# First heads' value products ahead of the next unit's update, with a VectorE fence behind the carried products

## The chip, the cores and the metric

One core of a Trainium2 chip runs the kernel. The metric is device time in microseconds of one execution. Engines are TensorE (PE for its matmuls, PEld for its weight loads), VectorE (DVE), ScalarE (ACT), GpSimd (POOL) and SyncE (SP, which here only issues DMAs). The granted clock is TensorE's, as the profile gives it.

## The reference

Retention attention (a causal, decaying linear attention without softmax) and then a gated linear unit whose gate is a causal convolution. Batch 8, 8 heads, 576 positions, head dimension 64, model width 512, five convolution taps; all inputs and the output are float32.

```python
scores = scale * np.matmul(q, k.transpose(0, 1, 3, 2))
Dmat = np.where(rel >= 0, gamma[:, None, None] ** rel[None, :, :], 0.0)
attn = np.matmul(scores * Dmat[None, :, :, :], v)
x = attn.transpose(0, 2, 1, 3).reshape(B, S, H * D)
...
for k in range(K):
    gate_pre += conv_w[k][None, None, :] * xp[:, k:k + S, :]
gate = 1.0 / (1.0 + np.exp(-gate_pre))
return gate * (x @ w_val) @ w_out
```

## The kernel before

The decay is taken apart: `gamma ** (i - j)` is a factor of the query row and one of the value row (`gin` on the values as they are cast, `gout` on the result), so what stands between the two matmuls is a plain 0/1 mask.

Work is cut into 18 units. Units 0 to 15 are "full": 256 positions of one batch element, two units to each element (`cu` is 0 or 1), each with two chunks `c` of 128 positions. Units 16 and 17 are "tail": the last 64 positions of four batch elements each. Heads are taken in pairs `pr` of 0 to 3; `hf` 0 means pairs 0 and 1 (the first heads), `hf` 1 pairs 2 and 3. Matmuls of a unit's attention use 64 x 64 quarters of the TensorE array, four after each other on four different quarters (`QUAD`).

For one unit the steps are:

- `turn_halves`: TensorE turns keys and queries, ScalarE copies them to `kq0` and `kq1`, one for each half of the heads.
- `scores(u, hf)`: 16 matmuls of a half into PSUM, in tile "s" for half 1, and in two tiles "v" for half 0.
- `masks(u, hf)`: VectorE multiplies by the mask into `p0` or `p1` (line 356 for one wide product, line 352 for two narrow ones, one for each "v" tile).
- `carried(u, odd)`: products of the queries with the state of the chunks before (`s1`, `s2` and the like), accumulated into the output banks `o0` and `o1`. A unit with `cu` 0 has no state for its chunk 0, so it makes half as many.
- `values(u, hf)`: 16 matmuls of `p` with the values of the heads of that half, accumulated into the same banks.
- `take_x`: VectorE multiplies the banks by `gout` and writes them to `xg`.
- `update(u)`: 32 short matmuls of keys and values into PSUM tile "s" (the bank that `scores` of half 1 had), ScalarE copies them out, and GpSimd adds them up to the next state (`states`).
- `conv`, `gate_values`, `project`, `store`: the convolution into tile "a" with its sigmoid on ScalarE, `value` (8 matmuls in each of two "v" tiles, written `v<-xg,wvb` in the profile) times the gate on VectorE, the output projection into "v" tiles, and the output DMA.

PSUM tile "v" has two buffers; "s", "a", "o0" and "o1" have one each. `p0` has two buffers, `p1` one.

The schedule is written by hand (`manual_schedule`): each engine runs its instructions in the order in which the program makes them, and semaphores are put in where tiles are shared. After a lead-in that differs, the loop at line 770 runs 14 phases, n = 4 to 17, each with parts of several units: the second half of unit n's scores and its values, the first half of unit n + 1's scores and its update, the gate and projection of unit n - 1, and loads, casts and turns of later units. `bring` issues loads, each behind a small copy on VectorE or ScalarE that touches the tile. Where the order of the program matters here:

- `carried(n, 1)` is made inside `scores(n, 1)`, after its first four matmuls.
- `masks(n, 1)` comes ahead of `masks(n + 1, 0)` on VectorE.
- `update(n + 1)` is made only where unit n + 1 is full, so in phases 4 to 14.
- `values(n, 1)` waits for `p1`; `values(n, 0)` needs only `p0`, which the phase before has made.

`fence` (line 398) is an existing helper that reads one column of an output bank; the lead-in uses it three times with VectorE. `fill` (line 151) makes small matmuls ahead of the loop until the count of matmuls stands at a given place in a block of 127.

Of the kernel before, what the change touches and what calls it, by code (L numbers as in the profile page):

```python
# [13 lines left out]
F32 = mybir.dt.float32  # L14
# [7 lines left out]
def kernel(  # L22
# [10 lines left out]
    nc = tc.nc  # L33
# [3 lines left out]
    P = 128  # L37
    NP = H // 2
# [22 lines left out]
    small = ctx.enter_context(tc.tile_pool(name="small", bufs=1))  # L61
# [7 lines left out]
    units = [("full", b, c) for b in range(B) for c in range(NC2)]  # L69
# [5 lines left out]
    half = (lo, hi)  # L75
    QUAD = ((0, 0), (1, 1), (0, 1), (1, 0))

    with tc.manual_schedule():
# [249 lines left out]
        def scores(u, hf, between=None, pool=None):  # L328

            if pool is ps_v:  # L330
                s = [pool.tile([P, 2, 2, P], F32, name="v") for par in range(2)]
            else:
                st = (pool or ps_s).tile([P, 2, 2, 2, P], F32, name="a" if pool else "s")
                s = [st[:, par] for par in range(2)]
            t = kqt[u][hf]
            for prl in range(2):
                for r in range(2):
                    for (c, par) in QUAD:
                        matmul(s[par][half[c], prl, r, :], lhsT=t[half[par], 0, prl, r, c, :],
                                         rhs=t[half[par], 1, prl, :, c, :],  # L340
                                         start=True, stop=True, skip_group_check=True)
                    if between and prl == 0 and r == 0:
                        between()
            sps[u, hf] = s if pool is ps_v else st

        def masks(u, hf):
            m = mask if units[u][0] == "full" else mask_t
            p = pp.tile([P, 2, 2, 2, P], BF16, name=f"p{hf}", bufs=2 - hf)
            mrow = m.rearrange("p r a -> p (r a)").unsqueeze(1)
            if isinstance(sps[u, hf], list):  # L350
                for par in range(2):
                    nc.vector.tensor_tensor(p[:, par].rearrange("p l r a -> p l (r a)"),  # L352
                                            sps[u, hf][par].rearrange("p l r a -> p l (r a)"),
                                            mrow.to_broadcast([P, 2, W]), op=ALU.mult)
            else:
                nc.vector.tensor_tensor(p.rearrange("p e l r a -> p (e l) (r a)"),  # L356
                                        sps[u, hf].rearrange("p e l r a -> p (e l) (r a)"),
                                        mrow.to_broadcast([P, 4, W]), op=ALU.mult)
            pt[u, hf] = p

        ops, state = {}, {}
        opened = set()

        def first(u, c, par):
            new = (u, c, par) not in opened
            opened.add((u, c, par))
            return new

        def out_banks(u):
            if u not in ops:  # L370
                ops[u] = [ps_o.tile([P, NP, P], F32, name=f"o{c}") for c in range(2)]
            return ops[u]

        def carried(u, odd, chs=(0, 1)):

            kind, b, cu = units[u]
            o = out_banks(u)
            for pr in range(NP):
                t = kqt[u][pr // 2]
                for c in chs:  # L380
                    par = c ^ odd
                    rows = half[par]
                    if kind == "full":
                        st = state.get((b, 2 * cu + c))
                        if st is None:
                            continue
                        matmul(o[c][rows, pr, :], lhsT=st[rows, pr, :],
                                         rhs=t[rows, 1, pr % 2, :, c, :],
                                         start=first(u, c, par), stop=False, skip_group_check=True)
                    else:  # L390
                        for i in range(2):
                            st = state[b + 2 * c + i, 4]
                            cs = slice(i * 32, i * 32 + 32)
                            matmul(o[c][rows, pr, :].rearrange("p (r a) -> p r a", r=2)[:, :, cs],
                                             lhsT=st[rows, pr, :], rhs=t[rows, 1, pr % 2, :, c, cs],
                                             start=first(u, c, par), stop=False, skip_group_check=True)

        def fence(u, rows, c, eng=None):
            t = small.tile([P, 1], F32, name="fence", bufs=2)
            (eng or nc.scalar.copy)(t[rows], ops[u][c][rows, NP - 1, 0:1])  # L400

        def values(u, hf):
            vb = bf[u]["v"]
            o = out_banks(u)
            p = pt[u, hf]
            for prl in range(2):
                pr = 2 * hf + prl
                for r in range(2):
                    for (c, par) in QUAD:
                        matmul(o[c][half[par], pr, :], lhsT=vb[half[c], 2 * pr + par, r, :],  # L410
                                         rhs=p[half[c], par, prl, r, :], start=first(u, c, par),
                                         stop=(r == 1), skip_group_check=True)
# [20 lines left out]
        def update(u, own=False, now=True):  # L433
            kind, b, cu = units[u]
            if kind != "full":
                return
            kb, vb = bf[u]["k"], bf[u]["v"]
            if own:
                xy = [ps_v.tile([P, 512], F32, name="v") for c in range(2)]
            else:  # L440
                xyt = ps_s.tile([P, 2, 512], F32, name="s")
                xy = [xyt[:, c] for c in range(2)]
            for pr in range(NP):
                for r in range(2):
                    for (c, par) in QUAD:
                        h = 2 * pr + par
                        matmul(xy[c][half[par], pr * 64:pr * 64 + 64], lhsT=kb[half[c], r, h, :],
                                         rhs=vb[half[c], h, r, :], start=(pr == 0 and r == 0), stop=(pr == NP - 1 and r == 1),
                                         skip_group_check=True)
            xf = stp.tile([P, 2, NP, 64], F32, name="xf")  # L450
            if own:
                for c in range(2):
                    nc.scalar.copy(xf[:, c].rearrange("p o d -> p (o d)"), xy[c][:, 0:NP * 64])
            else:
                nc.scalar.copy(xf.rearrange("p c o d -> p c (o d)"), xyt[:, :, 0:NP * 64])  # L455


            xfs[u] = xf
            if now:
                states(u)  # L460
# [130 lines left out]
        def gate_values(n, e):  # L591
            value(n, 0, e)
            gated(n, 0, e)
# [40 lines left out]
        warm(1, 512, ps_s)  # L634
        values(0, 1)
        fence(0, lo, 1, dve)
        turn(1, ps_v, 0)
        take_part(1, 0, act)
        take_x(0, (0,))
        carried(0, 1)  # L640
        carried(0, 0)
        turn(1, ps_v, 1)
# [127 lines left out]
        for n in range(4, NU):  # L770
            def bring(name, u, i, eng):
                if u < NU:
                    load_half(name, u, i, eng)

            nxt = n + 1 < NU
            carried(n, 0)
            scores(n, 1, lambda: carried(n, 1))
            masks(n, 1)
            conv(n - 1, 0)
            bring("v", n + 3, 0, act)  # L780
            if nxt:
                scores(n + 1, 0, pool=ps_v)
                masks(n + 1, 0)
                update(n + 1)
            bring("v", n + 3, 1, act)
            values(n, 1)
            values(n, 0)
            gate_values(n - 1, 0)
            bring("k", n + 3, 1, dve)
            gate_values(n - 1, 1)  # L790
            bring("q", n + 3, 1, dve)
            take_x(n, (0,))
            take_x(n, (1,))
            bring("k", n + 4, 0, dve)
            if n + 2 < NU:
                cast1("v", n + 2)
                cast_half("k", n + 2, 1)
                cast_half("q", n + 2, 1)
            if n + 3 < NU:
                cast_half("k", n + 3, 0)  # L800
                cast_half("q", n + 3, 0)
            if nxt:
                turn_halves((n + 1, 1), *([(n + 2, 0)] if n + 2 < NU else []))
            bring("q", n + 4, 0, act)
            project(n - 1, 0, 0, 2)
            project(n - 1, 0, 1, 2 - n % 2)
            store(n - 1)
# [34 lines left out]
```

## Time and profile before

| | us |
|---|---|
| Three runs: median (lowest to highest) | 160.12 (159.75 to 162.49) |
| The profiled execution, its own time | 159.02 |
| Its span in the profile | 157.3 |
| Its mean granted TensorE clock, share of full | 0.999 |
| The loop's first phase begins; the last one's convolution of unit 16 begins | 42.8; 140.6 |

Times in the profile count from the start of the span. In lists of groups and in the timeline a line reads: start, duration, engine, line of the kernel, operation, written tile <- read tiles, shapes, count, and in brackets the idle time of that engine before it with what ended it. All matmuls carry line 146, that of a helper that counts them, so they are told apart by their tiles: `o<-kq,s` are carried products, `s<-kq` and `v<-kq` scores of half 1 and half 0, `s<-vb,kb` the update, `o<-p,vb` the values. The chain of waits lists the work that ended last, in order of time. The list of waits reads: who waited, for whom, total us, times, longest.

### The profile page before, as it was taken

To read this page: it belongs to the slowest core of one execution; us is meant where nothing else is said; L and a number is where in the kernel's file an instruction comes from. 1 tells how busy PE (TensorE), PEld (TensorE's weight loads), DVE (VectorE), ACT (ScalarE), POOL (GpSimd) and SP (SyncE) were. 2 spreads that over 40 slices of the span, in tenths; PEclk is the share of its full clock that TensorE was granted. 3 is DMA by queue.
4 is the path that set the end of the run, shared out by engine and by line. 5 is a ranking of instruction groups with operands and counts; after the bars stand their busy time and mean duration, and the time that the engine had idled before them with its cause. 6 is when DMAs were issued, how large, how long until landed. Compare 5 with 4: busy or idle time off the path is not lost.

```text
span 157.3 us, 8008 instructions
## 1 busy us (share of the span) xinstructions
PE 145.8 (93%) x3461; PEld 115.3 (73%) x3461; DVE 105.2 (67%) x214; ACT 93.4 (59%) x164; POOL 102.4 (65%) x166
## 2 busy tenths in 40 slices
PE   6977989989999999999999999999999999998960
PEld 2456667868788878877878788887878887876720
DVE  5786887693676867667768686767667676765340
ACT  6895664697846574747484848484656637252510
POOL 7679669397969695959596877869695842500000
PEclk9999999999999999999999999999999999999999
DMA  4999999999989999998999899899778872302135
GB/s 117 347 347 342 324 290 333 325 310 308 351 276 292 300 352 363 321 315 234 305 264 314 249 322 285 262 314 267 213 230 241 262 236 108 137 17 121 36 101 133
DMA packets 62561, 40.37 MB, mean 257 GB/s; under 512 B 2346, under 2 KB 59710, under 8 KB 62526
## 3 DMA queue, kind: packets, MB, share of 16 engines
q1 hardware_dynamic: 62400, 39.59, 82.1%
q8 instruction: 27, 0.44, 1.2%
q10 hardware_dynamic: 126, 0.27, 0.7%
q14 instruction: 8, 0.07, 0.1%
HBM read 30.42 MB, written 9.44 MB: 253 GB/s over the span
## 4 chain that ended last, share of the span: by engine, by line
PE 80%; DVE 8%; DMA 3%; ACT 2%; issue 1%; SPq 1%; POOL 1%; POOLq 0%; DVEq 0%
PE v L146 45%; PE a L146 19%; PE o L146 10%; PE s L146 7%; DVE p L356 3%; DMA fv<-in_v_dram 2%; DVE p L352 2%; SPq L586 1%; DMA out_dram<-ob 1%; DVE z L547 1%; DVE kq L323 1%; ACT ob L562 1%; POOL wob L243 1%; DVE xg L421 1%; ACT gate L527 1%
## 5 line engine op out<-in xcount | busy, mean ns | idle before, releaser
L319 ACT COPY kq<-a 128x1024 bf16<-128x1024 bf16 x26 | 25.0, 1015 | 28.0 <-PE a L146 28.0
L146 PE MATMUL v<-xg,wvb 128*128 128x256 bf16 x288 | 34.8, 273 | 0.3
L146 PE MATMUL v<-wob,z 128*128 128x256 bf16 (+1 forms) x209 | 32.9, 305 | 1.2 <-POOL wob L243 0.6
L547 DVE TENSOR_TENSOR z<-gate,v 128x512 bf16<-128x512 f32 x34 | 23.3, 686 | 14.0 <-PE v L146 11.5
L356 DVE TENSOR_TENSOR p<-s,mask 128x1024 bf16<-128x1024 f32 x17 | 20.8, 1223 | 17.1 <-PE s L146 17.1
L146 PEld LDWEIGHTS <-wvb 128*128 128x128 bf16 x288 | 26.7, 97 | 5.2 <-issue 0.2
L264 POOL TENSOR_TENSOR vb<-fv,gin 128x512 bf16<-128x512 f32 x28 | 28.6, 1042 | 0.0
L146 PEld LDWEIGHTS <-z 128*128 128x128 bf16 x217 | 20.3, 98 | 9.2 <-issue 1.7
L421 DVE TENSOR_TENSOR xg<-o,gout 128x512 bf16<-128x512 f32 x32 | 22.3, 736 | 4.5 <-PE o L146 4.4
L527 ACT ACTIVATE gate<-a 128x1024 f32<-128x1024 f32 x17 | 17.4, 1024 | 12.6 <-ACT ob L562 6.7
L146 PE MATMUL a<-xg,dg 64*64 64x256 bf16 x720 | 24.3, 270 | 0.6 <-DVE xg L421 0.3
L562 ACT COPY ob<-v 128x512 f32<-128x512 f32 x34 | 18.6, 581 | 5.1 <-PE v L146 5.1
L146 PEld LDWEIGHTS <-dg 64*64 64x64 bf16 x720 | 20.0, 106 | 1.4 <-issue 0.7
L146 PEld LDWEIGHTS <-kb 64*64 64x64 bf16 (+1 forms) x656 | 15.9, 107 | 5.0 <-DVE p L356 2.0
L271 POOL CAST kb<-fk 128x512 bf16<-128x512 f32 x28 | 17.0, 612 | 0.1
L146 PEld LDWEIGHTS <-kq 64*64 64x64 bf16 x576 | 15.6, 106 | 2.0 <-issue 1.7
L352 DVE TENSOR_TENSOR p<-v,mask 128x512 bf16<-128x512 f32 x24 | 15.4, 685 | 1.0
L478 POOL TENSOR_TENSOR mid<-run,xf 128x256 f32<-128x256 f32 x8 | 5.8, 726 | 13.5 <-ACT xf L455 12.3
L271 POOL CAST qb<-fq 128x512 bf16<-128x512 f32 x22 | 13.5, 614 | 0.1
L146 PE MATMUL o<-p,vb 64*64 64x128 bf16 x576 | 12.3, 218 | 0.9 <-DVE p L356 0.5
L146 PEld LDWEIGHTS <-s 64*64 64x64 bf16 x256 | 8.2, 107 | 6.2 <-issue 3.4
L146 PE MATMUL s<-kq 64*64 64x128 bf16 x304 | 12.2, 222 | 0.4 <-DVE kq L323 0.3
(98 smaller groups left out, 197.2 us busy)
## 6 DMA issues: line engine op xcount, KB each, us to landing
out_dram<-ob SPq DMA_DIRECT2D x16, 512.0 KB, 4.5
fk<-in_k_dram SPq DMA_DIRECT2D x28, 256.0 KB, 4.5
fq<-in_q_dram SPq DMA_DIRECT2D x28, 256.0 KB, 4.6
fv<-in_v_dram SPq DMA_DIRECT2D x28, 256.0 KB, 4.6
wkc<-in_k_dram SPq DMA_DIRECT2D x2, 512.0 KB, 5.0
wqc<-in_q_dram SPq DMA_DIRECT2D x2, 512.0 KB, 5.5
wvc<-in_v_dram SPq DMA_DIRECT2D x2, 512.0 KB, 5.9
wvf<-in_moe_w_val_dram SPq DMA_DIRECT2D x4, 256.0 KB, 4.9
```

The costliest lines, as they stand in the source:

```text
L146: return f(*a, **k)
L243: eng(wob[:, o, :], wof[o])
L264: nc.gpsimd.tensor_tensor(b[n][:, hs].rearrange("p h r d -> p (h r) d"), f.rearrange("p h (r d) -> p (h r) d", r=2), gin[:, units[u][2], h ...
L271: (eng or nc.gpsimd.tensor_copy)(b[n][:, :, hs].rearrange("p r h d -> p h r d"), f.rearrange("p h (r d) -> p h r d", r=2))
L319: nc.scalar.copy(kqt[u][hf].rearrange("p i l r c a -> p (i l r c a)"), ps[:, at].rearrange("p i l r a -> p (i l r a)"))
L352: nc.vector.tensor_tensor(p[:, par].rearrange("p l r a -> p l (r a)"), sps[u, hf][par].rearrange("p l r a -> p l (r a)"), mrow.to_broadcas ...
L356: nc.vector.tensor_tensor(p.rearrange("p e l r a -> p (e l) (r a)"), sps[u, hf].rearrange("p e l r a -> p (e l) (r a)"), mrow.to_broadcast ...
L421: nc.vector.tensor_tensor(x[:, b, :, PAD + i0:PAD + i0 + P].rearrange("p o (a r) -> p o r a", r=2), o[c].rearrange("p o (r a) -> p o r a", ...
L478: nc.gpsimd.tensor_tensor(mid, state[b, "run"], xf[:, 0], op=ALU.add)
L527: nc.scalar.activation(t, cps[j, i], AF.Sigmoid)
L547: nc.vector.tensor_tensor(zsb[j][:, 2 * e + ss[0]:2 * e + ss[-1] + 1, :], gsb[j, i][e], vps[j, i, e], op=ALU.mult)
L562: (eng or nc.scalar.copy)(outs[u][:, r], o)
```

## The change

`carried` runs over the pairs and the chunks in reverse, so that its last product goes to pair 0. A new `fence_first(n)`, made between the scores and the masks of half 1, has VectorE copy one column of pair 0 of the bank and the partitions that this last carried product writes. In the loop, `values(n, 0)` moves from behind `values(n, 1)` to a place ahead of `update(n + 1)`. `carried` is used in the lead-in too; the fence and the move are in the loop alone.

```diff
-            for pr in range(NP):
+            for pr in reversed(range(NP)):
                 t = kqt[u][pr // 2]
-                for c in chs:
+                for c in reversed(chs):
                     par = c ^ odd
                     rows = half[par]
...
+        def fence_first(u):
+            c = 1 if units[u][0] == "full" and units[u][2] == 0 else 0
+            rows = half[1 - c]
+            t = small.tile([P, 1], F32, name="fence", bufs=2)
+            nc.vector.tensor_copy(t[rows], ops[u][c][rows, 0, 32:33])
...
             carried(n, 0)
             scores(n, 1, lambda: carried(n, 1))
+            fence_first(n)
             masks(n, 1)
             conv(n - 1, 0)
             bring("v", n + 3, 0, act)
             if nxt:
                 scores(n + 1, 0, pool=ps_v)
                 masks(n + 1, 0)
+            values(n, 0)
+            if nxt:
                 update(n + 1)
             bring("v", n + 3, 1, act)
             values(n, 1)
-            values(n, 0)
             gate_values(n - 1, 0)
```

## The prediction

> **What bounds the kernel now.** I read the page first: one core, granted clock full in all 40 slices, and TensorE (PE) holds the chain that ended last.
>
> ```profile
> PE 145.8 (93%) x3461; PEld 115.3 (73%) x3461; DVE 105.2 (67%) x214; ACT 93.4 (59%) x164; POOL 102.4 (65%) x166
> ...
> PE 80%; DVE 8%; DMA 3%; ACT 2%; issue 1%; SPq 1%; POOL 1%; POOLq 0%; DVEq 0%
> ```
>
> So only what TensorE waits for can be won, and anything that delays it is lost in full. Next came the waits between 43 and 140 us, where thirteen of the fourteen loop phases (n = 4 to 17) lie; two rows matter.
>
> ```profile
> PEld L146 <- issue: 4.5, 12, 0.4
> PEld L146 <- DVE p L356: 2.0, 11, 0.2
> ```
>
> The first is the step from the last 512-wide projection to the carried products (row by row, 11 of the 12) and is not touched. The second is the target: in each of the 11 phases that have an update (n = 4 to 14) the weight loads stand 0.18 us before it, because the update overwrites the bank that the mask product p1 of `masks(n, 1)` still reads. One phase, n = 6, in the timeline; the last line is from a later window of the same phase:
>
> ```profile
> 58.35 1.22 DVE L356 TENSOR_TENSOR p<-s,mask 128x1024 bf16<-128x1024 f32 x1 [1.20 <-PE s L146]
> ...
> 59.14 0.46 PE L146 MATMUL v<-kq 64*64 64x128 bf16 x16
> ...
> 59.62 0.33 PEld L146 LDWEIGHTS <-kb 64*64 64x64 bf16 x32 [0.18 <-DVE p L356]
> 59.62 0.45 PE L146 MATMUL s<-vb,kb 64*64 64x64 bf16 x32
> 59.66 0.69 DVE L352 TENSOR_TENSOR p<-v,mask 128x512 bf16<-128x512 f32 x1
> ...
> 60.45 0.28 PE L146 MATMUL v<-xg,wvb 128*128 128x256 bf16 x1
> ```
>
> p1 ends at 59.57 and the update starts 0.05 later. The line at 59.66 is the first half of `masks(n + 1, 0)`, call it pv1; it ends at 59.66 + 0.69 = 60.35. It frees the first of the two PSUM tiles "v", which the value product (v<-xg,wvb) at 60.45 needs. That second gate is 0.10 ahead of its user now. How close a user can follow, phase 16 shows, where there is no update (its chain):
>
> ```profile
> 134.56 0.02 issue
> 134.58 0.70 DVE p L352
> 135.29 0.04 issue
> 135.33 0.71 PE v L146 x5
> ```
>
> There the value product already waits for pv1, and starts 0.05 us after its end.
>
> **The weight-load row or the matmul row.** The matmul row hides most of this stall: the last score product runs to 59.60 and the update's first starts at 59.62, 0.02 us of idle PE a phase, 0.2 over 11 phases, against 2.0 by the weight loads. The Trainium skill, "Perfetto Trace Analysis", section "Identifying the Most-Contended Engine", says that matmul busy time is a bad measure since matmuls are pipelined, and that weight-load busy is the better one; the trace agrees (2.0 against 0.2), and by the matmul row alone the regular phases' term below would be at most 0.2.
>
> **The change part by part.**
> *Values first, update after.* In the new order TensorE has, after the scores of unit n + 1, 16 value products of the first heads that need only p0, written one phase earlier. Worked on phase 6: the last score product starts at 59.60 - 0.22 = 59.38; the 32 value products of now run 0.62 us, less the last one's 0.22, so 0.40 of issue, 0.20 a half. First half from 59.41 to 59.61; update from 59.62 (p1's release is 59.62 too) with 0.45 - 0.20 = 0.25 of issue, to 59.88; second half to 60.09; then the step to the value product, which takes 0.15 now (60.30 to 60.45): 60.24. TensorE alone would gain 60.45 - 60.24 = 0.21. But pv1 does not move: it starts 0.06 after the end (59.60) of the very score products that it masks, and those are ahead of the edit. So the value product starts at 60.35 + 0.05 = 60.40: a gain of 0.05, with 0.16 of slack left ahead of the gate. What is late next is pv1.
> Nine phases (4, 5, 6, 8 to 12, 14): 9 x 0.05 = 0.45.
> Phases 7 and 13 have besides a stall put down to nothing ("issue"), in 7 within the update, in 13 (0.14) at the start of the values:
>
> ```profile
> 67.19 0.26 PEld L146 LDWEIGHTS <-kb 64*64 64x64 bf16 x20
> 67.85 0.10 PEld L146 LDWEIGHTS <-kb 64*64 64x64 bf16 x1 [0.39 <-issue]
> 67.85 0.50 PEld L146 LDWEIGHTS <-vb 64*64 64x64 bf16 x32
> 68.44 0.11 PEld L146 LDWEIGHTS <-wvb 128*128 128x128 bf16 x2
> ```
>
> I read it as the instruction stream running dry (queue q8 carries 27 instruction transfers, and the kernel's own `fill` reckons with blocks of 127 matmuls): it then ends at 67.85 whatever the order. By the count it falls some 16 products earlier in the work, mid-update, so half an update, half the values and the step follow: 67.85 + 0.13 + 0.02 + 0.20 + 0.15 = 68.35 against 68.44. About 0.1 each, 0.2.
> Phases 15 and 16 have no update; their value product hangs on pv1 today: 0. Phase 17 has neither update nor pv1:
>
> ```profile
> 142.19 0.64 PE L146 MATMUL o<-p,vb 64*64 64x128 bf16 x32 [0.22 <-DVE p L356]
> ...
> 142.76 0.28 PE L146 MATMUL v<-xg,wvb 128*128 128x256 bf16 x1
> ```
>
> All 32 wait for p1 there; now 16 run ahead, and the value product comes at 142.19 + 0.20 + 0.15 = 142.54: 0.22.
> *The fence.* Fourteen VectorE copies of one column. The nearest row is the fence that the kernel has already, same shape, same banks (nanoseconds least, median, most; first and last start):
>
> ```profile
> L400 DVE COPY fence<-o x3: 129/134/151, 11.6 to 24.2; 64x1 f32<-64x1 f32 x3
> ```
>
> Behind it on VectorE stand p1, pv1 and the rest of the phase, and TensorE waits for p1 and pv1. The last carried product of phase 6 starts at 57.90 and ends at 58.12, so the fence runs 58.18 to 58.31; p1 cannot start before 58.35, when its scores release it, and VectorE is idle for 1.20 us before. Phase 7: 65.62 + 0.06 + 0.13 = 65.81 against 65.85. Cost 0 from below (it frees nothing). From above, if it is released only with the last score, 0.13 a phase on p1 and the update; the value product would still be ready at 60.24 + 0.13 = 60.37, under the gate's 60.40, and pv1's start at 59.66 has 0.09 (p1's end to pv1's start) plus the 0.08 by which back-to-back VectorE products overlap. I take 0; it costs from about 0.16 a phase on. The first half of the values waits for the fence, done 1.1 us before it is needed.
> *Reverse order of the carried products.* As many products; the first one now needs the second half of the turned queries, the second output bank free, and the newest state. In phase 7 it starts at 64.93; ScalarE's copy of that half ends near 64.33, `take_x` ends at 64.44, GpSimd's state is done at 63.0. Cover 0.5 us, cost 0; without it, at most the four or eight products that stood ahead, 0.1 a phase.
> *What moves with it.* `values` issues no DMA, so SP, ScalarE and GpSimd keep their order. The update ends at nearly the same time; its ScalarE copy waits for the gate activation anyway (59.49 + 1.03 = 60.52).
> Sum: 0.45 + 0.20 + 0.22 = 0.87 us. The profiled execution, 157.3 of span and 159.02 in all, becomes 158.15; the median of the runs shown is 160.12, 1.10 above it, and becomes 159.25, say **159.2**. That is 0.5%, where this kernel's runs (159.75 to 162.49) tell 2% from nothing.
>
> **Rivals.**
> A. *pv1 gates nothing* (the value product gets another tile, or pv1 starts earlier). Then nine phases give 0.21 each, 1.9; 7 and 13 0.2; 15 and 16 the 0.45 each that pv1 costs them; 17 0.22: 3.2 us, 156.9. For it, only that TensorE is ready; against it, phase 16. Chance 0.06.
> B. *The gate takes all*: the value product starts 0.10 after pv1 as today, the 0.15 step is paid after the gate, or the gain is lost among the runs. Only 17 is left: 159.9. Nothing in phases 15 and 16 speaks for it. Chance 0.17.
> C. *Slower: the instruction stream.* The crossing of phase 7 lies at nearly the same count in 5, 9, 11 and 13, and the new order reaches it about 0.13 us earlier (67.25 for 67.38). It decides if the instructions are then not there. A stall of 0.49 as in 7 costs 0.49 - 0.16 (slack to the gate) = 0.33 in 5, 9 and 11, and half as much in 13: 1.2 us, less the 0.87: 160.4. If the other crossings, in the convolution and the projection, begin to stall at 0.49 too, seven more cost 3.4: 163.8. Against: those in 5, 9 and 11 show no gap now. Chance 0.17, of it 0.05 for over 2%.
> D. *The fence is dear*: released later than the last score. At 0.45 a phase (0.29 past the slack, 14 times) 4.1 - 0.9 = 3.2 us slower, 163.3. Nothing shows such a wait. Chance 0.03.
> That the change does not do what it says: the order is written out by hand and the engines keep it, so no chance of its own.
>
> **How the numbers follow.** Forecast 0.57, A 0.06, B 0.17, C 0.17, D 0.03. The time is the forecast's. The range reaches from 158.0 (the forecast with twice the gain in 7, 13 and 17 and a run level like the profiled one's) to 160.9 (C without its far end, and half a us of run level); A and the ends of C and D are left out. Faster by over 2% (under 156.9): A, which lands on that bound, 0.05. Slower by over 2% (over 163.3): C's far end and D, 0.08. Within: 0.87.
>
> **What would show it.** Right: the waits of weight loads on p (L356) shrink from 2.0 us to near nothing in phases 4 to 14, and a wait on p (L352) appears ahead of the value product, as in 134.58; the period of a phase without issue stalls falls by about 0.05; the fence ends before p1's release, and p1's start after the last score stays at 0.06. Wrong: p1 later than that (D), value products starting well before pv1's end (A), gaps put down to issue in phases 5, 9 and 11 (C).

## The result and the profile after

The change made the kernel slower, by 3.3%: 166.6 us median (164.87 to 172.73, six runs) against 160.72 for the kernel before in as many (159.75 to 162.49), a ratio of 1.033 with a 95% interval of 1.026 to 1.041. Medians here and below are of all executions, ratios of those within 1.5% of each kernel's fastest. The profiled execution took 166.19 us, its span 164.4 against 157.3, 7.1 us more. The forecast was 159.2.

From the page of the changed kernel, the span, the busy times and the chain by engine:

```profile
span 164.4 us, 8017 instructions
PE 143.0 (87%) x3444; PEld 115.5 (70%) x3461; DVE 107.6 (65%) x228; ACT 93.9 (57%) x164; POOL 103.3 (63%) x166
...
PE 70%; DVE 12%; issue 7%; DMA 4%; SPq 1%; POOL 1%; ACT 1%; DVEq 0%; POOLq 0%
```

The weight loads are as many and as long as before, so TensorE has the same work. What is new is "issue" in the chain, 7% where it was 1%: time in which TensorE waits for nothing that the profile shows. The list of waits of the loop (43 to 147 us; who waited, for whom, total us, times, longest) says where:

```profile
PEld L146 <- issue: 11.9, 16, 1.9
...
PE s L146 <- issue: 4.2, 4, 1.4
...
PE o L146 <- issue: 1.8, 1, 1.8
PE v L146 <- issue: 1.4, 1, 1.4
...
PE v L146 <- DVE p L352: 0.4, 1, 0.4
PE a L146 <- issue: 0.3, 1, 0.3
```

The target is hit: the 2.0 us that weight loads stood for p (L356) are gone from the list. But matmuls stand 4.2 + 1.8 + 1.4 + 0.3 = 7.7 us for "issue". The kernel before has one such row in its loop (43 to 140 us):

```profile
PE s L146 <- issue: 0.3, 1, 0.3
```

The 7.4 us more cover the whole loss of span. Four of these gaps are in the update of the odd phases 7, 9, 11 and 13, one in the values of phase 15, one in the projection of phase 4. Phase 9 in the timeline:

```profile
85.14 0.20 PEld L146 LDWEIGHTS <-kb 64*64 64x64 bf16 x13
...
86.84 0.24 PEld L146 LDWEIGHTS <-kb 64*64 64x64 bf16 x19 [1.50 <-issue]
86.84 0.35 PE L146 MATMUL s<-vb,kb 64*64 64x64 bf16 x19 [1.39 <-issue]
```

The update stops behind its 13th matmul and goes on 1.5 us later. In the trace's order of weight loads the four gaps of phases 9 to 15 begin at numbers 1883, 2266, 2649 and 3032, each 383 apart: three blocks of 256 instructions, as a matmul is two instructions (766) and two more per pair of phases come in, of which below. The 27 instruction transfers on queue q8 (0.44 MB) are 16 KB each, and TensorE's 6940 instructions (3461 weight loads, as many matmuls, 18 semaphore instructions) make 27 blocks of 256. So, as far as the counts tell, TensorE waits for its instructions, which was rival C's place, with gaps two to four times the 0.49 us that it reckoned with.

An even phase shows the forecast at work. Phase 6 after the change:

```profile
60.32 1.23 DVE L356 TENSOR_TENSOR p<-s,mask 128x1024 bf16<-128x1024 f32 x1
...
61.34 0.22 PE L146 MATMUL o<-p,vb 64*64 64x128 bf16 x2
61.36 0.22 PE L146 MATMUL v<-kq 64*64 64x128 bf16 x1
61.38 0.42 PE L146 MATMUL o<-p,vb 64*64 64x128 bf16 x14
...
61.60 0.46 PE L146 MATMUL s<-vb,kb 64*64 64x64 bf16 x32
61.64 1.29 DVE L352 TENSOR_TENSOR p<-v,mask 128x512 bf16<-128x512 f32 x2
...
62.38 0.38 PE L146 MATMUL v<-xg,wvb 128*128 128x256 bf16 x2
```

From the start of the last score product (61.36) to the value product it is 1.02 us, where it was 60.45 - 59.38 = 1.07: 0.05 less, and the value product starts 0.05 behind pv1's end (61.64 + 0.69 = 62.33). Phases 8, 10, 12 and 14 show the same 1.02.

**Where the extra instructions come from.** At the first carried product of phase 9 the trace of the changed kernel has three waits: the weight load (82.90) waits for GpSimd, its matmul for ScalarE, and ahead of both a semaphore instruction of TensorE's sequencer (82.24) waits for VectorE. No weight load and no matmul in either trace waits for more than one engine.

In reverse order this product is the first to need three things at once: the newest state (GpSimd), the output bank (VectorE) and the second half of the turned queries (ScalarE). Forward, the first product needs only the state and the bank, one wait for the weight load and one for the matmul, and ScalarE's wait falls on a later product. The trace of before has no semaphore instruction of TensorE in the loop; this one has 11, at the start of phases 5 to 15 (50.47, 59.13, 66.40, 74.99, 82.24 and so on), each 0.45 to 1.7 us ahead of its carried product. Ten of them begin 0.04 us behind the end of `take_x` on VectorE (82.20 in phase 9): the sequencer was held until the output bank was free. The first comes later, behind the gap of phase 4. That gap, 1.4 of the 7.7 us, stands ahead of all 11, and they do not explain it. The page's count fits: 8017 - 8008 = 9 is 14 fences, these 11 and one more in the lead-in, less 17 matmul records that are missing.

**What happens to the instruction transfers.** Instruction DMAs in a stretch from just before the crossing in phase 8's projection, first of the kernel before (78.6 to 79.4), then of the changed one (80.7 to 84.3):

```profile
DMA packets 432, 0.23 MB, mean 286 GB/s; under 512 B 16, under 2 KB 431, under 8 KB 431
...
q8 instruction: 1, 0.02, 10.4%
```

```profile
DMA packets 1806, 0.92 MB, mean 257 GB/s; under 512 B 57, under 2 KB 1798, under 8 KB 1806
## 3 DMA queue, kind: packets, MB, share of 16 engines
q1 hardware_dynamic: 1806, 0.92, 85.6%
```

Before, the transfer starts within 0.8 us; after, there is none in 3.6 us. By the count of instructions, the crossings in the projections of phases 6, 8, 10, 12 and 14 were followed by the start of a transfer after 2.4, 0.6, 0.6, 0.6 and 0.5 us before, and after 2.9, 3.6, 3.1, 2.8 and 3.7 us with the change, 1.4 to 2.3 us behind the semaphore instruction that stands 10 matmuls past the crossing. The 0.6 us of before are at the low end, though: in the traces of experiments 1, 3, 6, 9 and 10, without a semaphore instruction just behind these crossings, the transfer started 0.4 to 3.0 us after them. With one there (the changed kernel, experiments 2 and 5) it was 2.8 to 4.0 us in 14 of 15 cases, and 1.0 us in one: in phase 10 of experiment 2 the transfer (103.50) started ahead of the semaphore instruction (103.97), and the update that followed had no gap. TensorE goes on 1.2 to 1.5 us after such a transfer's end (86.84 for one that ended at 85.36), and the next crossing is only 4.4 us of work further on, in the update.

### The profile page after: what moved, and what is told of

It reads as the page before. It is cut to its first block, busy times and chain, and to the rows that moved or that the text cites. A ratio compares the mean times of both kernels' runs of the same rounds, so it can differ in the third digit from the quotient of the medians.

```text
span 164.4 us, 8017 instructions
## 1 busy us (share of the span) xinstructions
PE 143.0 (87%) x3444; PEld 115.5 (70%) x3461; DVE 107.6 (65%) x228; ACT 93.9 (57%) x164; POOL 103.3 (63%) x166
## 3 DMA queue, kind: packets, MB, share of 16 engines
q1 hardware_dynamic: 62400, 39.59, 78.6%
## 4 chain that ended last, share of the span: by engine, by line
PE 70%; DVE 12%; issue 7%; DMA 4%; SPq 1%; POOL 1%; ACT 1%; DVEq 0%; POOLq 0%
PE v L146 39%; PE a L146 18%; PE o L146 8%; PE s L146 5%; DVE p L352 4%; DVE p L356 3%; DMA fv<-in_v_dram 2%; SPq L592 1%; DMA out_dram<-ob 1%; DMA cwn<-in_moe_conv_w_dram 1%; DVE dg L230 1%; DVE z L553 1%; DVE kq L323 1%; ACT ob L568 1%; POOL wob L243 1%
## 5 line engine op out<-in xcount | busy, mean ns | idle before, releaser
L146 PE MATMUL v<-wob,z 128*128 128x256 bf16 (+1 forms) x195 | 32.4, 299 | 3.6 <-issue 1.4
L146 PEld LDWEIGHTS <-wvb 128*128 128x128 bf16 x288 | 27.2, 97 | 5.6 <-issue 0.5
L356 DVE TENSOR_TENSOR p<-s,mask 128x1024 bf16<-128x1024 f32 x17 | 20.8, 1223 | 2.9 <-PE s L146 2.5
L146 PE MATMUL o<-p,vb 64*64 64x128 bf16 x576 | 15.7, 217 | 2.6 <-issue 1.8
L352 DVE TENSOR_TENSOR p<-v,mask 128x512 bf16<-128x512 f32 x24 | 15.4, 685 | 1.4 <-PE v L146 0.7
L146 PEld LDWEIGHTS <-vb 64*64 64x64 bf16 x576 | 11.4, 106 | 3.7 <-issue 3.4
L406 DVE COPY fence<-o 64x1 f32<-64x1 f32 x14 | 2.2, 157 | 17.0 <-PE s L146 14.3
```

The lines of the kernel that those rows point to most:

```text
L146: return f(*a, **k)
L406: nc.vector.tensor_copy(t[rows], ops[u][c][rows, 0, 32:33])
```

## Theories and experiments

*Theory W*: the semaphore instruction, which the reversed order brings, holds TensorE's sequencer just past a block's end, so the next block is asked for late. *Rival P*: the moved values put the crossing into the middle of the update, and that starves TensorE. *Rival F*: the fence on VectorE is what costs.

### 1. Forward order, values first

```diff
-            for pr in reversed(range(NP)):
+            for pr in range(NP):
...
-                for c in reversed(chs):
+                for c in chs:
...
-            nc.vector.tensor_copy(t[rows], ops[u][c][rows, 0, 32:33])
...
+            nc.vector.tensor_copy(t[lo], ops[u][1][lo, :, 32:33])
```

> Keeps the values ahead of the update and the fence, but carried runs forward again; the fence reads four cells (one for each pair) instead of one. Theory W (the reversed order puts two waits, VectorE and GpSimd, on the first carried weight load, the second one becomes a semaphore instruction that holds TensorE's sequencer, and the fetch of the next instruction block is asked for late): no such instruction in phases 5 to 15, issue gaps over 0.6 us in the loop vanish, 159 to 161 us. Rival P (values first moves the crossing between instruction blocks from the end of the update into its middle, and that starves TensorE): still 165 to 167 us with gaps of 1 to 2 us in the update of odd phases. Rival F (the fence on VectorE is what costs): still 165 to 167.

Measured: 159.97 us median, ratio to before 0.995 (0.989 to 1.001). Values first, the crossing mid-update and a fence are all still there, and the loss is gone: P and F fall. W's expectation that the gaps vanish missed, though: the profiled execution, the longest of its ten at 163.65, has seven of 0.7 to 1.5 us from weight load to weight load, three of them in the update of phases 7, 9 and 13, with no semaphore instruction in the loop. Its waits, over the whole span:

```profile
PE s L146 <- issue: 2.5, 3, 1.2
...
PE a L146 <- issue: 1.1, 1, 1.1
...
PE v L146 <- issue: 1.0, 2, 0.7
```

### 2. Reverse order alone

```diff
-            for pr in range(NP):
+            for pr in reversed(range(NP)):
...
-                for c in chs:
+                for c in reversed(chs):
```

(in the kernel before)

> The kernel before with the carried products reversed and nothing else: no fence, values behind the update. Theory W: 11 semaphore instructions on TensorE at the start of phases 5 to 15, fetches 1.3 to 2.3 us behind them, gaps of 1 to 2 us near the end of the update in odd phases: 164 to 167 us. Rivals P and F: nothing that they blame is there, 160 to 161.5 us.

Measured: 171.23 us (four runs), ratio 1.053 (1.041 to 1.066), more than the whole change costs. The weight loads of phase 7's update:

```profile
71.59 0.32 PEld L146 LDWEIGHTS <-kb 64*64 64x64 bf16 x29 [0.18 <-DVE p L356]
74.37 0.11 PEld L146 LDWEIGHTS <-kb 64*64 64x64 bf16 x3 [2.45 <-issue]
```

Both stalls stand side by side: the old one on p ahead of the update, and a gap of 2.45 us at the crossing near its end. 11 semaphore instructions are in the trace. The reverse order is enough for the loss.

### 3. The change whole, scores first

```diff
-            carried(n, 0)
-            scores(n, 1, lambda: carried(n, 1))
+            scores(n, 1, lambda: (carried(n, 0), carried(n, 1)))
```

> The changed kernel whole, but carried(n, 0) is made behind the first four score products of the phase, so that the waits for GpSimd and VectorE fall on different instructions; order of carried still reversed, fence and values as changed. Theory W: no semaphore instruction, 159 to 161.5 us. Rivals P and F: 165 to 167 us.

Measured: 160.42 us, ratio 0.990 (0.985 to 0.995). Here order, fence and values are as changed; only the waits are spread, since the first score products take ScalarE's. No semaphore instruction is left in the loop, and the waits (43 to 140 us) are those of a kernel that runs:

```profile
PE s L146 <- issue: 1.0, 3, 0.5
PE v L146 <- DVE p L352: 0.7, 2, 0.4
...
PE v L146 <- issue: 0.3, 1, 0.3
```

1.3 us for "issue" instead of 7.7. So it is not the reverse order as such that costs, but the wait that it puts on one instruction too many.

### 4. Blocks moved

```diff
-        BLOCK, PLACE = 127, 50
+        BLOCK, PLACE = 127, 70
```

> The changed kernel with 20 more small fill products ahead of the loop, so each crossing between instruction blocks falls 20 matmuls earlier in the work: the one in the projection goes from 12 to 32 matmuls ahead of the semaphore instruction, the one in the update into the values or scores just ahead. The semaphore instructions stay. Theory W: what counts is that the request for the next block stands close behind the crossing and is held; with 64 instructions between, it is no longer held: 160 to 162.5 us. If the held sequencer costs wherever the crossing lies: 164 to 167. Rival P: the crossing is still among short matmuls, 164 to 167.

Measured: 162.73 us, ratio 1.013 (1.008 to 1.018), just above W's range and below the other: with all 11 semaphore instructions in place, more than half of the loss goes when the crossing stands 30 matmuls ahead of them instead of 10 (by the trace's count of weight loads; the expectation has 32 and 12). In this trace four of the six transfers start ahead of the semaphore instruction. What is left are gaps of 1.4 us in the value products of phases 6 and 10, which had none.

### 5 and 6. Reverse order in half of the phases

```diff
+            back = u >= 4 and u % 2 == 1
-            for pr in reversed(range(NP)):
+            for pr in reversed(range(NP)) if back else range(NP):
...
-                for c in reversed(chs):
+                for c in reversed(chs) if back else chs:
```

(the second with `u % 2 == 0`; the fence reads four cells in the bank of the last product)

> The changed kernel, but carried runs in reverse only in the odd phases of the loop and forward elsewhere; the fence reads four cells, as in the run with the forward order. Six semaphore instructions on TensorE are left, at the start of phases 5, 7 to 15, each 12 matmuls behind the crossing in the projection. Theory W: these are the ones that hold the request of the next block, so most of the loss stays: gaps of 1 us or more in the update of odd phases, 163.5 to 167 us. Rival (each semaphore instruction costs the same, wherever it stands): about half of the loss, 162.5 to 164.

> The same with the reverse order only in the even phases from 6 to 16: five semaphore instructions, about 50 matmuls ahead of the crossing in the convolution and far from the one in the projection. Theory W: little is lost, at most some 0.3 us a pair of phases: 159.5 to 161.5 us. Rival (each one costs the same): 162 to 164.

Measured: odd phases 168.08 us (163.66 to 169.43, four runs) beside 161.55 for the kernel before; four runs are too few for an interval, but the lowest lies above 26 of the 29 of the kernel before. Even phases 160.21, ratio 0.991 (0.985 to 0.997). Six semaphore instructions behind the crossing cost as much as all 11, by these few runs, five that stand elsewhere nothing. So it is not their number that counts. That it is the place rests on experiment 4 too, since odd and even phases differ in more (the unit of an even phase has half as many carried products). The profiled executions took 168.94 and 161.34 us, both above their medians. Matmuls' waits in the loop, first of the odd, then of the even phases:

```profile
PE s L146 <- issue: 7.6, 5, 2.7
...
PE v L146 <- issue: 2.1, 1, 2.1
```

```profile
PE s L146 <- issue: 2.0, 4, 1.1
PE v L146 <- issue: 0.7, 1, 0.7
```

### 7 and 8. Blocks moved without the semaphore instructions

```diff
-        BLOCK, PLACE = 127, 50
+        BLOCK, PLACE = 127, 60
```

(in the variant of experiment 3, and in the kernel before)

> The variant with the scores first (no semaphore instruction, values ahead of the update), with 10 more fill products ahead of the loop. From its trace, 128 matmuls in a row then take at least 4.2 us between two crossings, where they take 3.3 to 3.9 now in the shortest of the three stretches. If what is left of the gaps is the fetch coming too late for the shortest stretch: gaps in the loop fall further, 158 to 159.5 us, and faster than the kernel before by 1.5 to 2.5%. If the place of the blocks does not matter once the sequencer is free: as without it, 0.99 of before.

> The kernel before with the same 10 more fill products and nothing else. If the place of the blocks matters by itself: 0.5 to 1% faster than before, the gaps in phases 7 and 13 go. If it gains as much as the variant with the change, the change has no gain of its own; by the timeline the change should be ahead of it by the 0.04 us of each regular phase and the 0.2 of phase 17, some 0.7 us. If not: 1.00.

Measured: 160.9 us, ratio 1.001 (0.997 to 1.005), and 161.21, ratio 1.004 (1.000 to 1.008). Both expectations of a gain missed. Longer stretches between crossings are worth nothing that can be seen once the sequencer is free, and moving the blocks costs nothing either; the gaps that remain (1.3 us in phase 7 of the second one's trace) come and go.

### 9 and 10. The order of the scores alone, and the variant again

In 9, the edit of experiment 3 in the kernel before; in 10, experiment 3 unchanged.

> The kernel before with carried(n, 0) behind the first four score products and nothing else (control for the variant with the scores first). If the gain of that variant (0.990, interval 0.985 to 0.995) is the values ahead of the update: 0.997 to 1.003 here, with the waits of weight loads on p (L356) of about 2 us in all still there. If it is the order of the scores: 0.99 here too.

> The variant with the scores first, unchanged, once more on the same chip as its control, since the version with other blocks came out at 1.00. Timeline: 0.04 us in each of 11 phases and 0.2 in phase 17, about 0.7 us, less what the gaps of the instruction stream take from run to run: 0.985 to 1.000.

Measured: 161.45 us, ratio 1.005 (1.001 to 1.010), and 160.33, ratio 0.998 (0.994 to 1.003). Scores first gains nothing by itself (the weight loads still stand 2.0 us for p in its trace), and the variant is some 0.7% ahead of this control (0.998 / 1.005), with intervals that overlap. The 1.0% of experiment 3 did not come again in full. The variant is ahead of the changed kernel; ahead of the kernel before it is by 0.2 to 1.0%, and the 0.2% is inside the noise.

## Why the prediction was wrong

- **Values first, update after: right.** 0.05 us in a regular phase was forecast for pv1's gate, 0.05 is there (phases 6, 8, 10, 12 and 14), and the value product waits for p (L352). Phase 17: from p1's start to the value product 149.82 - 148.19 = 1.63 us against 142.76 - 140.91 = 1.85, the 0.22 forecast. Phase 16 gained nothing, as forecast, and phase 15 nothing in experiment 3 (in the changed kernel it has a gap). The variants with values first and no held sequencer come out between 1.0% ahead and 0.1% behind (experiments 1, 3, 7 and 10), and only experiment 3's interval leaves out 1: the 0.5% of the sum fits them, but is not shown as a time.
- **The fence: right at nothing**, though it takes 161 ns instead of 134. In phase 6 p1 starts 0.28 us after the start of its last score product, as before; in the odd phases 0.31 against 0.27, which the slack ahead of pv1 hides.
- **Reverse order of the carried products: the step that failed.** "Cover 0.5 us, cost 0" counted whether the queries, the bank and the state are ready in time. They are, but it did not count the waits that the first product must carry. With one more than the weight load and the matmul hold, there is an instruction of the sequencer's own, and its price is not its wait but what stands behind it: the engine's run-ahead and, as the times of the transfers suggest, the request for the next block of instructions. Experiments 2 and 3 price this step at about 5% with nothing else changed, and at nothing with the waits spread.
- **Rival C: right place, wrong reason.** Its gaps were put down to a crossing reached 0.13 us earlier, at 0.33 us each. Experiment 1 keeps that earlier crossing and loses nothing by it in its median. Single gaps of its kind do come without any semaphore instruction, in both orders (1.1 and 1.0 us in phases 5 and 11 of experiment 9, values last; 1.6 in phase 5 of experiment 10, values first), so they are not tied to the earlier crossing. The gaps of the changed kernel measured 1.0 to 2.0 us, as the transfer started later: 2.2 to 3.2 us in phases 8 to 14, 0.5 in phase 6.
- **The gap that "ends at 67.85 whatever the order"**, a term for phases 7 and 13, did not hold: in phase 7 the gap was 0.50 us from weight load to weight load before, 1.2 after, and 1.0 in the trace of experiment 1, which has no semaphore instruction there.

The Trainium skill, "Perfetto Trace Analysis", section "Identifying Dependency Chains", says that an instruction that waits for several engines may get a semaphore instruction ahead of it; the trace agrees, with 11 in the loop. The Trainium skill, "Perfetto Trace Analysis", section "Per-engine timelines", has the sequencer push a matmul into a wait queue and go on, but finish a sequencer instruction, its wait included, before it takes the next. That fits the transfers that start behind it (84.41 for 82.24), though not the one of experiment 2 that started ahead. Both were there to be read before the prediction.

That the sequencer's hold delays the request is argued from the times of the transfers and from the place (experiments 4 to 6); no record shows the request itself. What experiment 4 leaves at 1.3%, the gap of phase 4, and the gaps that vary from run to run without any semaphore instruction, stay open.

## What to carry to other kernels

When a step is reordered, count for its new first instruction on how many engines it now waits, not only whether they are done: one wait more than a weight load and its matmul can hold became an instruction of the sequencer's own here, and the sequencer stood there until that wait was over. On an engine with thousands of instructions, look at where such a stop stands against the ends of instruction blocks; spread the waits over neighbours (here, four score products first). And gaps marked "issue" that stand a whole number of instruction blocks apart were fetches here: their size went with the lateness of a transfer, not with the work around them.

## What the hardware showed that was not expected

A stop of the sequencer cost nothing by itself (five in the even phases: 0.991 of before) and 3 to 5% where stops stood 10 matmuls behind a block's end (1.033 for the change, 1.053 for the reverse order alone). From the end of a 16 KB instruction transfer to the first instruction of the block went 1.2 to 1.5 us, in the kernel before too (66.48 to 67.85 in phase 7).
